# Agent values at a batch's end: the chain cut into five steps, with VectorE's part of each half moved behind other work

## The chip, the cores and the metric

The kernel runs on one core of one Trainium2 chip (trn2). The metric is the device time of one launch in microseconds. Before the change the median of three timed runs is 715.16 us (714.91 to 716.64).

## What is computed

The reference is agent attention followed by a mixture of experts. Four batches of N = 11456 rows of C = 128 numbers (q, k and v) and 49 agents a batch:

```python
a2k = sm(agents, k)              # softmax over the N keys, scale 1/sqrt(128)
agent_v = a2k @ v                # 49 x 128 a batch: the "agent values"
q2a = sm(q, agents)              # softmax over the 49 agents
x = (q2a @ agent_v).reshape(B * N, C)
do_compute = x @ w_skip > 0      # the other rows keep x
e_idx = argmax(x @ w_gate)       # one of 8 experts a row, gate_w its softmax weight
y = gate_w * (relu(x @ w1[e]) @ w2[e])
out = x + y where do_compute else x
```

`agent_v` of a batch needs all keys and values of that batch, and every query of the batch needs `agent_v`. So there are four points, one at each batch's end, at which a short serial chain (`agent_values`) turns a sum in PSUM into the matrix `av` that the queries are multiplied with.

## The kernel before

**Two parts.** `attention` (about the first 312 us of the profile) works through 60 chunks, 15 a batch, of up to six columns of 128 rows each. `experts` (from about 345 us on) runs the gathered rows through the eight experts, one block of 384 rows at a time. The change touches `attention` alone.

**Slots.** `attention` is emitted as a list of 79 slots (0 to 78), and each engine runs its instructions in exactly the order in which they are emitted. In a slot of the steady state one chunk of queries goes through (scores `sQ`, maximum `qS`, exponential `qE`, transpose `qT`, product with `av` `mX`, division `qN`, gate `qG`, weight `qD`, output `qO`, each some slots behind the other), and in the same slots the keys (`sK`, `kC`, `kM`, `vS`, `vE`) and values (`vA`) of the next batch. A slot has up to two key chunks (the first half of a batch) or two to three value chunks (the second half). The table `ORDER` says in which order a slot emits these stages, with one row a phase: "k" and "v" for batch 0's keys and values, "w" for slots 10 to 55, "q" for the last batch's queries from slot 56 on.

**Words that step helpers.** Some chains are Python generators in a list `back`; the word `bg` of a row advances each of them by one step, up to its next `yield`. Before, `bg` stands twice in a "w" slot and once in a "q" slot. Two sorts of generator matter here: `agent_values`, and `early`, which looks up rows for the experts and shares its slots with batch 2's chain. The word `rt` advances the routing work (`codes`, `count`, `routing`: the VectorE instructions named `best`, `code`, `mask`, `cum`, `oin`, `n`).

**The chain** `agent_values(b)` has three steps before. Step 1, called at once when the last value chunk is emitted (`vA`, slots 10, 25, 40 and 55): two VectorE copies `pa<-ps_a` (L432) of the summed products. Step 2, in the next slot's first `bg`: TensorE's product with `pairs` (L435) adds the two halves, and VectorE copies the result to `at` (L437). Step 3, in the second `bg` of that slot (a "q" slot later for batch 3): three TensorE products (L440 to L442) into a PSUM tile `pv`, then VectorE's sum, reciprocal and two scalings (L445, L446, L449) that write `av`.

```python
vec.tensor_copy(pa[h : h + NA, :], st["A"][h : h + NA, : C + 1])
yield
ten.matmul(pt[:, :P], lhsT=pa[:, :C], rhs=pairs, start=True, stop=True)
vec.tensor_copy(at, pt[:, :P])
yield
ten.matmul(pv[:, :C], lhsT=at, rhs=ident, start=True, stop=True)
```

**Names in the rows.** `ps_s` are the three PSUM tiles of scores, `qm` (L456) is VectorE's maximum over a query chunk, `qe` (L462) ScalarE's exponential of it, which frees the `ps_s` tile, `eT` (L472) ScalarE's copy of the transposed exponentials (L470), `ps_x` (L483) the product with `av`, and L491, L499 the division on VectorE that ends in `xs` and `G`. `top` (L520) on VectorE, a subtraction on GpSimd (L521) and `best` (L551) on VectorE belong to the gate. `ps_e` are two PSUM tiles that the transposes and the chain share. Loads go through SyncE's queue into 13 buffers (`ld`, `more`, `lds`).

Of the kernel before, what the change touches and what calls it, by code (L numbers as in the profile page):

```python
# [44 lines left out]

ORDER = {
# [4 lines left out]
}  # L51


# [121 lines left out]
def attention(nc, tc, sh, io, ps):  # L175


    q, k, v, agents, w_skip, w_gate, w1, w2, flat = io
# [6 lines left out]
    chunks = [(b, ci) for b in range(sh.B) for ci in range(NCH)]  # L185
    with ExitStack() as ctx:
# [4 lines left out]
        rt = ctx.enter_context(tc.tile_pool(name="rt", bufs=1))  # L191
# [50 lines left out]
        while at < sh.NC:  # L242
            n = next((n for n in range(1, sh.NC - at) if sh.COLS[at + n] != sh.COLS[at] + n), sh.NC - at)
# [57 lines left out]
        def raw(e, i):  # L301

            src = w2[e].rearrange("(f p) d -> p f d", p=P) if i else w1[e]
            to = ps.raw[e][i].rearrange("p (f d) -> p f d", d=C) if i else ps.raw[e][i]
            behind(nc.sync.dma_start(out=to, in_=src), room(e))
# [40 lines left out]
        def weights(n):  # L346

            e, i = n
            tl, r = taken(("w", n))
            if i < 2:  # L350
                hi, lo = (x[:, i * 512 : (i + 1) * 512].rearrange("p (a b) -> p a b", b=C) for x in ps.w1[e])
            else:
                hi, lo = (x[:, (i - 2) * 4 : (i - 1) * 4, :] for x in ps.w2[e])
            r.append(act.copy(hi, tl))
            r.append(pool.tensor_tensor(out=lo, in0=tl, in1=hi, op=ALU.subtract))
            del held["w", n]
            yield
# [56 lines left out]
        def values(n):  # L414


            b, ci, cols, m = geometry(n)
            x = stored(n)
            tl, r = taken(("v", n))
            if ci == 0:  # L420
                st["A"] = ps_a.tile([P, 512], F32, name="ps_a")
            for t in range(m):
                h = 64 * (t % 2)
                r.append(ten.matmul(st["A"][h : h + NA, : C + 1], lhsT=x[:, t, :], rhs=tl[:, t, :],
                                    start=(ci == 0 and t < 2), stop=(ci == NCH - 1 and t >= m - 2)))
            st["last"] = r
            del held["v", n]

        def agent_values(b):

            for h in (0, 64):
                vec.tensor_copy(pa[h : h + NA, :], st["A"][h : h + NA, : C + 1])  # L432
            yield
            pt = ps_e.tile([P, 512], F32, name="ps_e")
            ten.matmul(pt[:, :P], lhsT=pa[:, :C], rhs=pairs, start=True, stop=True)  # L435
            at = one.tile([P, P], F32, name="at")
            vec.tensor_copy(at, pt[:, :P])  # L437
            yield
            pv = ps_e.tile([P, 512], F32, name="ps_e")
            ten.matmul(pv[:, :C], lhsT=at, rhs=ident, start=True, stop=True)  # L440
            ten.matmul(pv[:, C : C + NE + 1], lhsT=at, rhs=wgs, start=True, stop=True)
            ten.matmul(pv[:, W - 1 : W], lhsT=pairs, rhs=pa[:, C:], start=True, stop=True)  # L442
            rs = one.tile([P, 1], F32, name="rs")
            av = avs[b % 2]
            vec.tensor_scalar(rs, pv[:, W - 1 : W], EPS, None, op0=ALU.add)  # L445
            vec.reciprocal(rs, rs)  # L446
            for h in (0, 64):
                s = slice(h, h + NA)
                vec.tensor_scalar(av[s, : W - 1], pv[s, : W - 1], rs[s], None, op0=ALU.mult)  # L449
            st["av", b] = av  # L450
# [354 lines left out]
        def static(upto):  # L805

            n = 0
            while st["items"] < upto:
                f, *args = items[st["items"]]
                n += f in (rows, layer1, first_result)  # L810
                waits = {layer2: (layer1, *args), first_result: (sums, 0)}.get(f)
                if n > 2 or any(i == waits or f in (rows, layer1) and i[0] is rows for i, _ in open_):
                    return
                g = iter(f(*args))
                if next(g, True) is None:
                    open_.append(((f, *args), g))
                st["items"] += 1
# [11 lines left out]
        def goal(kind, i):  # L829
            lst = {"k": sh.K, "v": sh.V, "q": range(1 - sh.Q0, n_all + 1)}[kind]  # L830
            return max(0, lst[min(i, len(lst) - 1)]) if i >= 0 else 0
# [12 lines left out]
        def prefetch(i):  # L844
            nonlocal pos
            while pos < len(order) and order[pos][0] < i + 8:
                bufs = few + (i < late + PAR["few"][0]) * rooms + (i < late + PAR["few"][1]) * many[-PAR["more"] :]
                if not free(bufs):
                    break
                load(order[pos][1], bufs)  # L850
                pos += 1

        back, fresh, queue = [], [], []

        def step(lst, n=None):
            for g in lst[:n]:
                if next(g, True):
                    lst.remove(g)
# [13 lines left out]
        def values_done(n):  # L872
            assert done["vE"] > n
            values(n)
            if chunks[n][1] == NCH - 1:
                begin(agent_values(chunks[n][0]))

        def begin(g):
            next(g)
            fresh.append(g)  # L880
# [30 lines left out]
        def held_up(x, n):  # L911
            return ("mb", chunks[n][0]) not in st if x == "vS" else done["vS"] <= n
# [9 lines left out]
        with tc.manual_schedule(engines=None):  # L922
            for i in range(slots):
                prefetch(i)
                back += fresh
                fresh.clear()
                at = i - sh.Q0
                phase = "k" if i < -(-NCH // PAR["first"]) + 1 else "v" if at < 0 else "w" if i < sh.LATE else "q"
                if at in EARLY:
                    assert st["routed"] >= 0  # L930
                    back.append(early(EARLY[at]))
                for n in starts.get(i, []):
                    wgen.append(weights(n))
                for n in raws.get(i, []):
                    raw(*n)
                for word in ORDER[phase].split():
                    x, soft, lag = word[:2], word.endswith("?"), int(word[2:].strip("?") or 0)
                    if x == "bg":
                        step(back)
                    elif x == "rt" or x == "rx" and at >= n_all - 4:  # L940
                        step(queue, 1)
                    elif x == "wt":
                        step(wgen)
                    elif x == "rx":
                        pass
                    elif x == "sa":
                        static(STATIC.get(at - n_all, len(items) if at > n_all else 0))
                    elif x in ("sr", "sx"):
                        for pair in open_[:]:
                            if next(pair[1], True) or x == "sx":  # L950
                                open_.remove(pair)
                    else:
                        kind, f = stages[x]
                        to = goal(kind, i - lag)
                        if x == "kM" and goal(kind, i + 1) % NCH == 0:
                            to = goal(kind, i)
                        while done[x] < to and not (soft and held_up(x, done[x])):
                            f(done[x])
                            done[x] += 1
            assert all(x == n_all for x in done.values()) and not open_ and st["items"] == len(items), done  # L960
            back += fresh
            assert not wgen
            while back:
                step(back)
            while queue:
                step(queue, 1)
# [566 lines left out]
def build(nc, args, out, n):  # L1533
    sh = Shapes(args[0].shape[0], n)
    ps = Persist(nc, sh)
    io = args + [out]
    with tile.TileContext(nc) as tc:
        attention(nc, tc, sh, io, ps)
    experts(nc, sh, out, ps)
# [32 lines left out]
```

## Time and profile before

| what | before |
|---|---|
| median of three timed runs | 715.16 us |
| fastest and slowest of them | 714.91, 716.64 us |
| the profiled execution's own time | 708.03 us |
| its span, first to last instruction | 706.5 us |
| TensorE matmul busy | 630.2 us (89%) |
| VectorE busy | 518.1 us (73%) |
| ScalarE busy | 359.8 us (51%) |
| GpSimd busy | 194.5 us (28%) |
| mean granted TensorE clock | 0.948 |

Busy times are of the span of the profiled execution. In the rows below PE is TensorE's matmuls, PEld its weight loads, DVE VectorE, ACT ScalarE, POOL GpSimd and SP SyncE. "[2.16 <-PE ps_a L424]" behind a row means that the engine sat idle for 2.16 us just before it and that a TensorE instruction of line 424 ended the wait. The granted clock is given as a share: 1.00 is 2.4 GHz and 0.50 is 1.2 GHz. Line numbers in these rows are those of the kernel before; in the changed file those behind L435 are one or two higher.

### The profile page before, as it was taken

What the parts mean: (1) busy time and instruction counts of PE and PEld (TensorE: products, weight loads), DVE (VectorE), ACT (ScalarE), POOL (GpSimd) and SP (SyncE); (2) the same over time, 40 slices, a digit from 0 to 9 for tenths busy, and PEclk for the clock granted to TensorE, in tenths of its full rate; (3) what the DMA queues carried; (4) which work ended last, traced back from release to release, by engine and by line L of the source; (5) the groups of instructions that cost most, each with busy time, mean ns of one, the idle gap of its engine ahead of it and who ended that gap; (6) DMA issues with size and microseconds to landing.
All of it is one profiled execution on the core that took longest, in us unless ns stands there. A gap on an engine that the chain in (4) does not pass through costs nothing. (4 is left out here: it accounts for less than half of the span.)

```text
span 706.5 us, 21190 instructions
## 1 busy us (share of the span) xinstructions
PE 630.2 (89%) x6808; PEld 583.9 (83%) x6808; DVE 518.1 (73%) x1854; ACT 359.8 (51%) x1024; POOL 194.5 (28%) x322
## 2 busy tenths in 40 slices
PE   6599898798888979977787999999999999999985
PEld 6588787687777867766676899999999999999985
DVE  4527568876877688876555878888888888888884
ACT  3336565465344545642434455555555555555552
POOL 2302440252234412145554531111111101011253
PEclk9799999989797989997999999999999999999998
DMA  8999899999797999621121101111111111111100
GB/s 315 358 360 375 287 402 404 401 308 404 271 343 256 372 379 318 233 101 48 43 42 36 35 29 47 46 47 46 47 46 46 35 37 44 47 46 52 42 25 5
DMA packets 56760, 119.69 MB, mean 169 GB/s; under 512 B 12902, under 2 KB 21226, under 8 KB 56624
## 3 DMA queue, kind: packets, MB, share of 16 engines
q1 hardware_dynamic: 42064, 79.92, 32.1%
q10 hardware_dynamic: 8928, 23.79, 8.6%
q0 software_dynamic: 5632, 14.53, 6.6%
q14 instruction: 95, 0.78, 0.4%
q8 instruction: 41, 0.67, 0.4%
HBM read 87.18 MB, written 31.50 MB: 168 GB/s over the span
## 5 line engine op out<-in xcount | busy, mean ns | idle before, releaser
L1308 ACT ACTIVATE hh<-h 128x384 fp32r<-128x384 f32 x296 | 143.7, 491 | 107.6 <-ACTq L996 101.4
L1243 DVE SCALAR_TENSOR_TENSOR hl<-h,hh 128x384 fp32r<-128x384 f32 x296 | 155.3, 552 | 41.8 <-DVEq L996 30.9
L1484 PE MATMUL y<-hh,w 128*128 128x384 f32 x592 | 160.0, 351 | 15.4 <-PEq L996 14.5
L1478 PE MATMUL h<-xh,w 128*128 128x384 f32 x592 | 154.0, 342 | 4.4 <-PEq L996 4.4
L1484 PEld LDWEIGHTS y<-hh,w 128*128 128x128 f32 x592 | 102.7, 190 | 20.4 <-issue 20.2
L1478 PEld LDWEIGHTS h<-xh,w 128*128 128x128 f32 x592 | 108.9, 191 | 5.5 <-issue 5.5
L1478 PE MATMUL h<-xl,w 128*128 128x384 f32 x296 | 101.1, 342 | 0.0
L1484 PE MATMUL y<-hl,w 128*128 128x384 f32 x296 | 100.3, 339 | 0.0
L462 ACT ACTIVATE qe<-ps_s,qm 128x49 f32<-128x49 f32 x360 | 75.2, 308 | 39.2 <-DVE qm L456 34.5
L1354 POOL DMA_DIRECT2D xg<-out_dram x29 | 15.8, 543 | 203.2 <-issue 203.1
L483 PE MATMUL ps_x<-av,eT 50*128 50x138 f32 x720 | 62.0, 307 | 8.2 <-DVE G L499 8.0
L483 PEld LDWEIGHTS ps_x<-av,eT 50*128 50x128 f32 x720 | 49.5, 196 | 19.8 <-issue 9.1
L366 PE MATMUL ps_s<-agT,ld 128*64 128x49 f32 x1296 | 50.8, 236 | 11.5 <-DMA ld<-in_k_dram 5.6
L366 PEld LDWEIGHTS ps_s<-agT,ld 128*64 128x64 f32 x1296 | 45.9, 150 | 17.2 <-issue 12.5
L499 DVE TENSOR_TENSOR xs<-ps_x,qr 128x768 f32<-128x768 f32 x60 | 57.5, 959 | 3.5 <-DMA out_dram<-xs 0.6
L1478 PEld LDWEIGHTS h<-xl,w 128*128 128x128 f32 x296 | 56.6, 191 | 0.0
L1484 PEld LDWEIGHTS y<-hl,w 128*128 128x128 f32 x296 | 55.8, 189 | 0.0
L1304 ACT ACTIVATE yT<-y 128x384 f32<-128x384 f32 x37 | 18.1, 491 | 65.8 <-ACTq L996 58.9
L407 POOL TENSOR_TENSOR scores<-scores,mb 128x294 f32<-128x294 f32 x53 | 41.6, 811 | 29.1 <-DVE mb L401 24.7
L374 ACT COPY scores<-ps_s 128x294 f32<-128x294 f32 x60 | 23.9, 420 | 43.3 <-PE ps_s L366 35.3
L366 PE MATMUL ps_s<-agT,lds 128*64 128x49 f32 x1056 | 41.2, 231 | 5.0 <-issue 2.9
L366 PEld LDWEIGHTS ps_s<-agT,lds 128*64 128x64 f32 x1056 | 36.6, 145 | 10.0 <-issue 5.7
(200 smaller groups left out, 1005.5 us busy)
## 6 DMA issues: line engine op xcount, KB each, us to landing
out_dram<-xs ACTq DMA_DIRECT2D x60, 387.0 KB, 6.9
ld<-in_q_dram SPq DMA_DIRECT2D x29, 384.0 KB, 7.4
ld<-in_k_dram SPq DMA_DIRECT2D x25, 384.0 KB, 7.8
lds<-in_v_dram SPq DMA_DIRECT2D x24, 387.0 KB, 6.6
lds<-in_k_dram SPq DMA_DIRECT2D x23, 384.0 KB, 7.5
lds<-in_q_dram SPq DMA_DIRECT2D x21, 384.0 KB, 7.3
ld<-in_v_dram SPq DMA_DIRECT2D x20, 387.0 KB, 6.4
more<-in_v_dram SPq DMA_DIRECT2D x16, 387.0 KB, 7.2
```

Source lines behind the costliest of these rows:

```text
L366: r.append(ten.matmul(pt[h : h + 64, t * NA : (t + 1) * NA], lhsT=xT[:, t * P + h : t * P + h + 64], rhs=agT[:, b, :], start=True, stop=True))
L374: act.copy(stored(n), s)
L407: eng.tensor_tensor(out=x, in0=x, in1=st["mb", chunks[n][0]].unsqueeze(1).to_broadcast(x.shape), op=ALU.subtract)
L462: act.activation(qes[n % PAR["qe"]][:, t, :NA], s[:, t, :], AF.Exp, bias=mx[:, t : t + 1])
L483: ten.matmul(px[:, h, t, :], lhsT=eT[s, t * P : (t + 1) * P], rhs=st["av", b][s, :], start=True, stop=True)
L499: vec.tensor_tensor(out=out, in0=px[:, :, :, w], op=ALU.mult, in1=rs.unsqueeze(3).to_broadcast(list(px[:, :, :, w].shape)))
L1243: v.scalar_tensor_tensor(out=hl[:, f], in0=h_ps[f % HB], scalar=0.0, in1=hh[:, f], op0=ALU.max, op1=ALU.subtract).then_inc(sem["HL"], 1)
L1304: s.activation(yT, y_ps, AF.Copy).then_inc(sem["YS"], 1)
L1308: s.activation(hh[:, f], h_ps[f % HB], AF.Relu).then_inc(sem["HH"], 1)
L1354: g.dma_start(out=xg[n % TURN].rearrange("p h c -> p (h c)"), in_=in_rows(n)).then_inc(x, 16)
L1478: w = t.matmul(h_ps[f % HB], lhsT=ps.w1[e][wx][:, cs], rhs=x, start=(n == 0), stop=(n == 2))
L1484: w = t.matmul(y_ps, lhsT=ps.w2[e][wx][:, f, :], rhs=h[:, f], start=(f == 0 and n == 0), stop=(f == FC - 1 and n == 2))
```

## The change

`agent_values` gets two more `yield`s, so that it has five steps: copies to `pa`; the `pairs` product; the copy to `at`; the three products into `pv`; `av`. A new word `be` at the place of the last `bg` of a "v", "w" or "q" slot also takes up chains that were put into a new list `ended`. The chain is put there when the last value chunk is emitted, and no longer started at once. So step 1 comes at the end of its slot, TensorE's steps at the next two slots' `bg`, and VectorE's steps at the same slots' `be`. In the "q" row `bg` moves ahead of `qS`, and `be` takes its old place.

```diff
-    "w": "qN+4 sK kC vS-1? qD+5 sQ+1 vA vE-1? bg qS+1 qG+4 qE+1 kM+1 rt qT+2 qO+5 mX+3 bg vS-1 vE-1 rt wt",
-    "q": "sr qN+4 qD+5 sQ+1 sx qS+1 sa qG+4 qE+1 bg qT+2 rt qO+5 mX+3 rt rx wt",
+    "w": "qN+4 sK kC vS-1? qD+5 sQ+1 vA vE-1? bg qS+1 qG+4 qE+1 kM+1 rt qT+2 qO+5 mX+3 be vS-1 vE-1 rt wt",
+    "q": "sr qN+4 qD+5 sQ+1 sx bg qS+1 sa qG+4 qE+1 be qT+2 rt qO+5 mX+3 rt rx wt",
...
             ten.matmul(pt[:, :P], lhsT=pa[:, :C], rhs=pairs, start=True, stop=True)
+            yield
             at = one.tile([P, P], F32, name="at")
             vec.tensor_copy(at, pt[:, :P])
             yield
...
             ten.matmul(pv[:, W - 1 : W], lhsT=pairs, rhs=pa[:, C:], start=True, stop=True)
+            yield
             rs = one.tile([P, 1], F32, name="rs")
...
-                begin(agent_values(chunks[n][0]))
+                ended.append(agent_values(chunks[n][0]))
...
                     if x == "bg":
+                        step(back)
+                    elif x == "be":
+                        back += ended
+                        ended.clear()
                         step(back)
```

No instruction is added or dropped. ScalarE's, GpSimd's and SyncE's orders stay as they are; TensorE's and VectorE's change at the four batch ends.

VectorE at batch 2's end (slot 40), before. `ehit` and `want` are of `early`, `qm` is the next query chunk's maximum, `best` is of the gate:

```order
L499 TENSOR_TENSOR G<-ps_x,qr 128x2x3x9
L432 COPY pa<-ps_a 49x129 x2
L700 TENSOR_SCALAR ehit<-iota,rank,rec 128x128 x3
L703 TENSOR_SCALAR want<-rank,rec 128x3
L704 TENSOR_TENSOR want<-want,rank 128x3
L456 TENSOR_REDUCE qm<-ps_s 128x6
L520 TENSOR_REDUCE top<-G 128x12
L551 SCALAR_TENSOR_TENSOR best<-G,desc 128x192
```

and with the change:

```order
L501 TENSOR_TENSOR G<-ps_x,qr 128x2x3x9
L702 TENSOR_SCALAR ehit<-iota,rank,rec 128x128 x3
L705 TENSOR_SCALAR want<-rank,rec 128x3
L706 TENSOR_TENSOR want<-want,rank 128x3
L458 TENSOR_REDUCE qm<-ps_s 128x6
L522 TENSOR_REDUCE top<-G 128x12
L553 SCALAR_TENSOR_TENSOR best<-G,desc 128x192
L432 COPY pa<-ps_a 49x129 x2
```

The copies that need the summed values have moved from ahead of `qm` to behind `best`. For batches 1 and 3 it is the same; for batch 0 they stay where they are.

TensorE in the two slots after batch 2's end (41 and 42), before; `ps_s` products are scores, `qe` transposes:

```order
L366 MATMUL ps_s<-agT,lds 64x49 x36
L435 MATMUL ps_e<-pairs,pa 128x128
L470 MATMUL ps_e<-ident,qe_110 128x128 x3
L483 MATMUL ps_x<-av_159,eT 128x138 x6
L440 MATMUL ps_e<-ident,at 128x128
L441 MATMUL ps_e<-wgs,at 128x9
L442 MATMUL ps_e<-pa,pairs 128x1
L366 MATMUL ps_s<-agT,lds 64x49 x12
L366 MATMUL ps_s<-agT,ld_95 64x49 x12
L366 MATMUL ps_s<-agT,lds 64x49 x12
```

and with the change:

```order
L366 MATMUL ps_s<-agT,lds 64x49 x36
L435 MATMUL ps_e<-pairs,pa 128x128
L472 MATMUL ps_e<-ident,qe_110 128x128 x3
L485 MATMUL ps_x<-av_159,eT 128x138 x6
L366 MATMUL ps_s<-agT,lds 64x49 x12
L366 MATMUL ps_s<-agT,ld_95 64x49 x12
L366 MATMUL ps_s<-agT,lds 64x49 x12
L441 MATMUL ps_e<-ident,at 128x128
L442 MATMUL ps_e<-wgs,at 128x9
L443 MATMUL ps_e<-pa,pairs 128x1
```

The three products that need `at` have moved behind the next slot's three groups of scores.

VectorE in slot 42, with the change (`run` is the keys' running maximum, `oin` and `n` are of the routing):

```order
L385 TENSOR_TENSOR run<-scores,run 128x294 x2
L577 MEMSET oin_3020 128x1
L578 COPY oin_3020<-cum_2941 128x8
L580 TENSOR_TENSOR n_3023<-oin_3020 128x8
L447 TENSOR_SCALAR rs<-ps_e 128x1
L448 RECIPROCAL rs<-rs 128x1
L451 TENSOR_SCALAR av_158<-ps_e,rs 49x137 x2
L553 SCALAR_TENSOR_TENSOR best<-G,desc 128x96
```

Before, the three rows that write `av` stood a slot earlier, behind the last row of `early` and ahead of the scan `cum`.

## Rows read from the trace of the kernel before

**Rows 1.** Busy time by stretch: length, PE, PEld, DVE, ACT, POOL busy, clock, DMA share, GB/s

```profile
103.50:170.00 66.50, 59.46 (x1143) 51.84 (x1141) 51.17 (x160) 36.53 (x144) 19.49 (x41) 0.95 1.00 376
170.00:246.00 76.00, 66.94 (x1146) 57.68 (x1143) 58.65 (x207) 36.46 (x142) 28.74 (x49) 0.87 0.89 319
345.00:706.00 361.00, 339.56 (x2045) 330.73 (x2043) 278.73 (x1083) 189.47 (x402) 83.95 (x109) 0.98 0.14 40
```

**Rows 2.** Timeline, VectorE's part of the chain: start us, length us, instruction [idle before]

```profile
43.42 0.60 DVE L432 COPY pa<-ps_a 49x129 f32<-49x129 f32 x2 [8.92 <-PE ps_a L424]
45.92 0.29 DVE L437 COPY at<-ps_e 128x128 f32<-128x128 f32 x1 [1.91 <-PE ps_e L435]
103.57 0.60 DVE L432 COPY pa<-ps_a 49x129 f32<-49x129 f32 x2 [1.60 <-PE ps_a L424]
108.13 0.29 DVE L437 COPY at<-ps_e 128x128 f32<-128x128 f32 x1 [0.45 <-PE ps_e L435]
110.13 0.16 DVE L445 TENSOR_SCALAR rs<-ps_e 128x1 f32<-128x1 f32 x1 [0.49 <-PE ps_e L442]
170.17 0.60 DVE L432 COPY pa<-ps_a 49x129 f32<-49x129 f32 x2 [2.16 <-PE ps_a L424]
177.37 0.29 DVE L437 COPY at<-ps_e 128x128 f32<-128x128 f32 x1 [1.13 <-PE ps_e L435]
181.06 0.16 DVE L445 TENSOR_SCALAR rs<-ps_e 128x1 f32<-128x1 f32 x1 [1.44 <-issue]
245.95 0.59 DVE L432 COPY pa<-ps_a 49x129 f32<-49x129 f32 x2 [1.45 <-PE ps_a L424]
```

**Rows 3.** Timeline, what stands behind the chain at batch 2's end

```profile
166.53 1.61 PE L366 MATMUL ps_s<-agT,ld 128*64 128x49 f32 x48
171.90 0.46 DVE L456 TENSOR_REDUCE qm<-ps_s 128x6 f32<-128x294 f32 x1
172.99 0.36 DVE L551 SCALAR_TENSOR_TENSOR best<-G,desc 128x192 bf16<-128x192 f32 x1 [0.47 <-POOL G L521]
174.48 2.13 PE L366 MATMUL ps_s<-agT,lds 128*64 128x49 f32 x48 [1.83 <-ACT qe L462]
```

**Rows 4.** Busy time by stretch of 4 us, columns as in rows 1

```profile
112.00:116.00 4.00, 2.71 (x61) 2.31 (x59) 3.78 (x13) 1.62 (x7) 0.50 (x1) 1.00 1.03 407
172.00:176.00 4.00, 2.17 (x66) 2.05 (x61) 3.35 (x13) 2.51 (x10) 0.67 (x3) 0.92 1.03 414
176.00:180.00 4.00, 4.00 (x31) 3.32 (x30) 2.33 (x12) 1.63 (x7) 0.09 (x1) 0.50 0.97 364
184.00:188.00 4.00, 3.81 (x65) 3.17 (x63) 3.79 (x16) 1.16 (x7) 1.24 (x2) 0.80 0.53 174
```

**Rows 5.** Timeline, TensorE's waits at the ends of batches 0, 1 and 3

```profile
46.27 0.49 PE L440 MATMUL ps_e<-ident,at 128*128 128x128 f32 x2 [0.38 <-DVE at L437]
114.09 0.97 PE L483 MATMUL ps_x<-av,eT 50*128 50x138 f32 x12 [1.29 <-DVE G L499]
249.52 0.55 PE L470 MATMUL ps_e<-ident,qe 128*128 128x128 f32 x3 [0.97 <-ACT eT L472]
```

**Rows 6.** Timeline, the same TensorE work, one chunk's scores, at either clock

```profile
171.75 0.91 PE L366 MATMUL ps_s<-agT,lds 128*64 128x49 f32 x24
182.27 1.49 PE L366 MATMUL ps_s<-agT,ld 128*64 128x49 f32 x24
```

**Rows 7.** Loads: two key loads' issue in SyncE's queue, and their kind's median time to landing

```profile
158.50 2.22 SPq L336 DMA_DIRECT2D lds<-in_k_dram  x2
...
lds<-in_k_dram SPq DMA_DIRECT2D x23, 384.0 KB, 7.5
```

**Rows 8.** Timeline, batch 2's `av`, routing's `n`, and the first product with that `av`

```profile
181.45 0.74 DVE L449 TENSOR_SCALAR av<-ps_e,rs 49x137 f32<-49x137 f32 x2
187.50 0.17 DVE L578 TENSOR_TENSOR n<-oin 128x8 bf16<-128x8 f32 x1
190.54 0.98 PE L483 MATMUL ps_x<-av,eT 50*128 50x138 f32 x12
```

More of the change, by code (lines that the diff above doesn't have):

```diff
@@ L851, in prefetch @@
                 pos += 1
-        back, fresh, queue = [], [], []
+        back, fresh, ended, queue = [], [], [], []
         def step(lst, n=None):
```

2 rows, old and new, of the table ORDER are left out of this document.

## The prediction

> **What bounds the kernel now.** I read the busy time by stretch first. The experts' part (the last row of [rows 1]) is TensorE's, 339.56 us busy of 361, and the change does not touch it: whatever attention gains or loses shifts this part as a whole. In attention no engine is alone at its limit: from 103.5 to 170 us TensorE is busy 59.46 us of 66.5 and VectorE 51.17, with transfers at 376 GB/s; the next batch takes 76 us, at a mean clock of 0.87 instead of 0.95. So I looked at the four batch ends for the wait that ends last.
>
> The timeline of VectorE shows it [rows 2]. At each batch's end VectorE comes to the two copies to `pa` and sits idle until TensorE has finished the value products: 8.92, 1.60, 2.16 and 1.45 us for batches 0 to 3. It runs its instructions in order, so what stands behind the copy waits too. At batch 2 that is `qm`, the query chunk's maximum. Its scores are among the 48 products that begin at 166.53 and take 1.61 us, so they are there by 168.2; `qm` starts at 171.90 [rows 3]. ScalarE's exponentials wait for `qm`, the `ps_s` tile is free only after them, and TensorE stands still for 1.83 us until 174.48 "<-ACT qe". Then the clock falls: 1.00 before, 0.92 over 172 to 176, where TensorE is busy 2.17 us of 4, and 0.50, the 1.2 GHz level, from 176 to 180 [rows 4].
>
> **The change, part by part.** Nothing is added, so every term is a wait that goes or a piece of work that lies elsewhere. The sum is made against the profiled execution (708.03 us); the timed median is 715.16, 7.13 us or 1% above it, which no row explains, and I carry the difference over as it is. A gain of one slot counts once, since all later slots follow.
>
> *Copies to `pa` behind `best`, batches 1 to 3.* VectorE gets to `qm` without the wait. By the time `best` is done, TensorE has ended the value products, so the wait goes and is not put off: at batch 2 VectorE is free at 168.0 (170.17 less 2.16). `ehit` and `want` take the 1.1 us between the copies' end (170.77) and `qm` (171.90), `qm` 0.46, and `top`, GpSimd's subtraction and `best` the 1.0 us up to 173.35 [rows 2, 3]: it reaches the copies at about 170.6, 0.4 us after TensorE let them go.
>
> *`pairs` and `at` parted.* The copy to `at` waits 1.91, 0.45, 1.13 and 0 us now [rows 2], none for batch 3, since TensorE's product comes only just before it. Behind `qm`, `run`, `code` and `mask` it has no wait left. TensorE's products that need `at` move behind three groups of scores, 2.7 us at full clock (3 x 0.91, [rows 6]), so TensorE is no longer kept by `at` either.
>
> *`av` at the end of the next slot.* The waits of 0.49 and 1.44 us ahead of L445 [rows 2] go the same way. The work itself, 0.16 + 0.16 + 0.74, some 1.1 us, stays and lies a slot later. The `ps_e` tile that holds `pv` is kept about a slot longer; only a transpose two tiles on needs it, and that one stands behind a slot of scores, so I cost it at nothing (if that cover failed, 1 to 2 us a batch).
>
> *The word moved in "q".* It touches batch 3's chain alone: the three `pv` products go ahead of a static block's transposes. Nothing waits for either there; 0.
>
> The terms, batch by batch:
> - Batch 0: the copies stay. TensorE's own wait for `at`, 0.38 us [rows 5], goes. Bounds 0 and 1.91 (all of VectorE's wait for `pairs`). I take **0.4**, TensorE's row, since VectorE idles 8.92 us just before and is no limit there.
> - Batch 1: VectorE's waits are 1.60 + 0.45 + 0.49 = 2.54 us. Part of it VectorE will spend on waiting for TensorE's scores and products instead, since it comes to them earlier. TensorE has a wait of 1.29 us on VectorE's `G` in the same slots [rows 5]. Bounds 0 and 2.54; I take **1.2**, just under the nearest row, 1.29.
> - Batch 2: VectorE's waits are 2.16 + 1.13 + 1.44 = 4.73 us, and VectorE is the limit afterwards (3.79 us busy of 4 from 184 to 188, [rows 4]), so what it saves is worth most here. On TensorE's side the stall is 1.83; without it the clock need not fall, and at 0.50 a chunk's scores take 1.49 us instead of 0.91 [rows 6]: the two chunks left of slot 41 and the three of slot 42 lose 5 x 0.58 = 2.9 us, and with the transposes and products among them I put the slow stretch at 3.3 us, an estimate. Bounds 1.8 (the stall alone) and 4.73. I take the middle, **3.3**, because both engines must be early for a slot to be early, and the clock's share is not certain.
> - Batch 3: VectorE's wait is 1.45 us, TensorE waits 0.97 us for `eT` in the slot behind [rows 5], which hangs on `qm` in the same way. Bounds 0 and 1.45; **0.9**, by TensorE's row.
>
> Sum: 0.4 + 1.2 + 3.3 + 0.9 = **5.8 us**: 702.2 us for a profiled execution like this one, 715.16 - 5.8 = **709.4 us** for the median.
>
> **The rivals.**
>
> *The slow stretch comes anyway.* From 112 to 116 us TensorE is busy 2.71 us of 4 and the clock stays at 1.00; from 172 to 176 it is busy 2.17 and the clock falls [rows 4]. So it is a matter of degree, and the profiled run and the timed ones differ by 1%, more than this whole term. If the clock falls there all the same, batch 2 gives back what the low level costs and keeps some 1.0 us: 0.4 + 1.2 + 1.0 + 0.9 = 3.5, **711.7 us**. The Trainium skill (TensorE: Matmul & The Clock Gate, section on the clock gate) says that the monitor behind the clock runs on a beat of its own that is not tied to the kernel, and that the same kernel meets it at another point from run to run. By that rule the 3.3 us is a draw and not a saving. One trace cannot show it; the two rows above do not contradict it.
>
> *The transfers hide it.* At 112 to 116 and 172 to 176 the transfer engines are busy throughout (share 1.03) at 407 and 414 GB/s, the most in these rows. If data were the limit, an earlier VectorE would only wait for loads: no gain, **715.2 us**. For it speaks that share; against it, that the two key loads issued from 158.50 on are read at 171.75 and 174.48, 13 us after their issue, where the median to landing is 7.5 [rows 3, 6 and 7], and that the rate falls to 174 GB/s from 184 to 188 [rows 4], with buffers full.
>
> *`av` comes too late (slower).* Now batch 2's `av` is done at 182.19, and its first use, a product on TensorE, is at 190.54: 8.4 us of room [rows 8]. With the change `av` stands behind `n`, which ends at 187.67, and takes 1.1 us: at the pace of before 188.8, 1.7 us ahead of its use. If VectorE, the limit in that slot, falls more than 1.7 us behind TensorE, the product waits, the scores behind it wait in TensorE's order, and the clock may fall as it did at 174. For batches 1 and 2 a stall of 2 us and a slow stretch of 3.3 each make 10.6, less 5.8 gained: **720 us**. Against it speaks that everything ahead of `av` on VectorE also comes earlier, by more than 1.7 us at batch 2.
>
> That the change does not do what it says can be left aside: the orders show each row moved as described.
>
> **How the numbers follow.** I give my forecast 0.53, the slow stretch that comes anyway 0.14, the transfers 0.21 and the late `av` 0.12. About 0.3%, 2.1 us, is what a measurement of this kernel can tell from no change. The first two lie below 713.0, so faster is 0.67; the third is within it, same 0.21; the fourth slower, 0.12. The range: all upper bounds together are 1.91 + 2.54 + 4.73 + 1.45 = 10.6 us, 704.5; upward it takes in the case of the transfers with the scatter of the runs before, which reaches 1.48 us above their median: 716.5. The late `av` is left out.
>
> **What would show it.** In the profile of the changed kernel, `pa` of batches 1 to 3, `at` and L447 (the old L445) should have no idle time worth naming ahead of them; that of batch 0's `pa` stays near 8.9 us. The stall of 1.83 us "<-ACT qe" behind batch 2's end should be gone and the clock there be 1.00; the stretch from batch 2's end to batch 3's (170 to 246 now) should be shorter by some 3 us, the one before it by about 1, and the experts' part unchanged. I am wrong if VectorE's idle time goes and the batch ends do not move (transfers, or TensorE), if a low clock turns up at another place, or if the first product with a new `av` waits for it.

## The result, and the profile after

| what | before | after |
|---|---|---|
| median, first comparison | 715.28 us (714.91 to 716.64, 4 runs) | 705.06 us (704.27 to 706.48, 4 runs) |
| the profiled execution's own time | 708.03 us | 704.27 us |
| its span | 706.5 us | 702.7 us |
| mean granted TensorE clock | 0.948 | 0.949 |

The ratio is 0.990, with a 95% interval of [0.986, 0.9939]. Two later comparisons, with more runs, gave 0.9917 [0.9889, 0.9945] (705.74 against 712.21 us) and 0.9906 [0.9877, 0.9934] (705.43 against 712.46 us). So the change gains about 6 to 7 us. (The ratios are not the quotients of the two medians and differ from them by up to 0.003.) The 10.2 us between the first two medians also hold a draw of the kernel before: over 34 runs of it in a later comparison the median is 712.5 us, and the time went from 706.89 us, at a mean clock of 0.958, to 715.91 us, at 0.935. Runs more than 1.5% above the fastest of their kernel are left out of the ratios; here that is a 35th run of 717.78 us.

The timeline of VectorE in the changed kernel answers to [rows 2]; L438 and L447 are the old L437 and L445:

```profile
42.39 0.60 DVE L432 COPY pa<-ps_a 49x129 f32<-49x129 f32 x2 [7.93 <-PE ps_a L424]
50.12 0.16 DVE L447 TENSOR_SCALAR rs<-ps_e 128x1 f32<-128x1 f32 x1 [1.46 <-PE ps_e L443]
103.53 0.60 DVE L432 COPY pa<-ps_a 49x129 f32<-49x129 f32 x2 [0.46 <-PE ps_a L424]
108.38 0.28 DVE L438 COPY at<-ps_e 128x128 f32<-128x128 f32 x1
112.89 0.15 DVE L447 TENSOR_SCALAR rs<-ps_e 128x1 f32<-128x1 f32 x1
168.02 0.59 DVE L432 COPY pa<-ps_a 49x129 f32<-49x129 f32 x2
173.78 0.28 DVE L438 COPY at<-ps_e 128x128 f32<-128x128 f32 x1
179.22 0.15 DVE L447 TENSOR_SCALAR rs<-ps_e 128x1 f32<-128x1 f32 x1
179.61 0.74 DVE L451 TENSOR_SCALAR av<-ps_e,rs 49x137 f32<-49x137 f32 x2
238.95 0.60 DVE L432 COPY pa<-ps_a 49x129 f32<-49x129 f32 x2
```

The waits of 1.60, 2.16 and 1.45 us ahead of the copies are 0.46, 0 and 0, and those ahead of `at` and `rs` of batches 1 and 2 are gone. Batch 0 keeps its long wait, and ahead of its `rs` VectorE waits 1.46 us, where it waited 0.33 before; the last section shows what TensorE did there. TensorE's timeline behind batch 2's end answers to [rows 3]:

```profile
165.69 2.16 PE L424 MATMUL ps_a<-more,scores 128*49 128x129 f32 x36
...
169.45 2.32 PE L366 MATMUL ps_s<-agT,lds 128*64 128x49 f32 x72
...
182.32 0.97 PE L485 MATMUL ps_x<-av,eT 50*128 50x138 f32 x11
...
186.47 1.17 PE L366 MATMUL ps_s<-agT,more 128*64 128x49 f32 x24 [1.61 <-ACT qe L464]
```

The three groups of scores of slot 41 are one row now, without the 1.83 us ahead of the second. A stall "<-ACT qe" of 1.61 us comes further on, in slot 44. The kernel before has one at the same place, shorter, and its clock stays at 1.00 from 188 to 196 us:

```profile
193.54 0.91 PE L366 MATMUL ps_s<-agT,more 128*64 128x49 f32 x24 [1.19 <-ACT qe L462]
```

The busy time of the same stretches as in [rows 4] (PE, PEld, DVE, ACT, POOL, then clock, DMA share and GB/s):

```profile
172.00:176.00 4.00, 3.50 (x83) 3.07 (x83) 3.81 (x13) 2.34 (x9) 1.84 (x1) 1.00 1.03 399
176.00:180.00 4.00, 3.53 (x64) 3.01 (x59) 3.74 (x18) 1.32 (x8) 1.88 (x3) 1.00 1.03 404
184.00:188.00 4.00, 2.39 (x61) 2.27 (x62) 3.73 (x15) 2.39 (x10) 0.97 (x2) 0.87 1.03 389
```

The clock is 1.00 where it was 0.92 and 0.50. From 184 to 192 us it falls instead, behind the 1.61 us stall: 0.87 in the last row, and 0.71 from 188 to 192. VectorE is busy 3.7 to 3.8 us of every 4: from the end of the copies on it has next to no idle time until 188 us. The experts' part does the same work; this stretch of 361 us begins 6.8 us earlier, as its first block does:

```profile
338.20:699.20 361.00, 340.49 (x2052) 332.34 (x2051) 279.63 (x1084) 190.47 (x405) 82.92 (x108) 0.99 0.13 40
```

But it is not as long as before. The stretch in [rows 1] ends 0.5 us ahead of the end of the span, this one 3.5 us. From the start of the first block, shown below, to the end of the span the profiled execution of the kernel before took 378.7 us and that of the changed kernel 381.6; the twelve further executions in this document, one of them of the kernel before, took 381.0 to 383.2. So the execution that the prediction was worked out from was some 3 us short in a part that no edit touches. This is why the profiled executions lie only 3.8 us apart although attention ends 6.8 us earlier. Of these 6.8 us, 1.0 lie ahead of batch 0's end (41.21 against 40.19 below), where nothing was changed.

To see which batch's end gave what, I take the start of TensorE's last value products of each batch as a milestone. In the kernel before, by its timeline:

```profile
41.21 2.16 PE L424 MATMUL ps_a<-ld,scores 128*49 128x129 f32 x36
...
102.03 1.49 PE L424 MATMUL ps_a<-ld,scores 128*49 128x129 f32 x24
...
167.96 2.16 PE L424 MATMUL ps_a<-more,scores 128*49 128x129 f32 x36
...
243.75 2.16 PE L424 MATMUL ps_a<-lds,scores 128*49 128x129 f32 x36
...
327.83 0.98 PE L1478 MATMUL h<-xh,w 128*128 128x384 f32 x2 [2.83 <-PEq L996]
```

and in the changed one:

```profile
40.19 2.16 PE L424 MATMUL ps_a<-ld,scores 128*49 128x129 f32 x36
...
101.99 1.49 PE L424 MATMUL ps_a<-ld,scores 128*49 128x129 f32 x24
...
236.75 2.16 PE L424 MATMUL ps_a<-lds,scores 128*49 128x129 f32 x36
...
321.07 0.98 PE L1484 MATMUL h<-xh,w 128*128 128x384 f32 x2 [2.58 <-PEq L1002]
```

The differences of these starts, with the same ones from the profiles of the experiments below (one execution each):

| profile | batch 0 to 1 | 1 to 2 | 2 to 3 | 3 to first expert block |
|---|---|---|---|---|
| before | 60.82 | 65.93 | 75.79 | 84.08 |
| before, once more (e1_same) | 59.43 | 65.30 | 77.88 | 82.49 |
| after | 61.80 | 63.70 | 71.06 | 84.32 |
| after, once more (e8_after) | 59.44 | 66.97 | 70.33 | 84.21 |
| after, once more (e13_after) | 60.19 | 64.37 | 73.29 | 83.93 |
| copies alone (e2_pa) | 61.31 | 64.77 | 72.30 | 83.71 |
| copies alone (e12_pa) | 59.78 | 66.39 | 73.03 | 84.08 |
| copies alone, batch 2 alone (e9_pa2) | 59.35 | 67.53 | 71.44 | 85.23 |
| whole change, batch 2 alone (e4_b2) | 61.12 | 65.86 | 72.98 | 85.35 |
| whole change, batches 1 to 3 (e6_b123) | 61.91 | 62.12 | 73.39 | 83.80 |
| five steps alone (e3_five) | 61.76 | 64.45 | 74.86 | 84.63 |
| stall filled (e5_fill) | 61.41 | 64.39 | 75.21 | 82.96 |

Equal code differs by up to 3.3 us in the second column between two executions, so one row of it proves little. The third column is clear: with the copies of batch 2 moved it is 70.33 to 73.39, without 74.86 to 77.88. (The two experiments that move the look-ups are left out.)

A shorter stretch has less scatter. From the start of slot 40's query scores to the start of slot 42's it is 16.3 and 17.0 us in the two executions of the kernel before, and 9.8 in each of the three of the changed one; 10.5 to 10.6 with the copies alone, 13.4 with the five steps alone, 12.6 with the stall filled. To slot 46's it is 36.7 and 38.6 us before, 32.1, 32.2 and 33.7 after; 32.3 to 33.7 with the copies alone, 35.3 with the five steps alone, 35.9 filled. At batch 3's end the query scores of slots 55 and 57 begin, before:

```profile
243.02 0.91 PE L366 MATMUL ps_s<-agT,lds 128*64 128x49 f32 x24
...
250.90 0.91 PE L366 MATMUL ps_s<-agT,ld 128*64 128x49 f32 x24
```

and after:

```profile
236.02 0.91 PE L366 MATMUL ps_s<-agT,lds 128*64 128x49 f32 x24
...
242.71 0.91 PE L366 MATMUL ps_s<-agT,ld 128*64 128x49 f32 x24
```

That is 7.9 and 6.7 us. Of the executions in the table, every one without batch 3's copies moved has 7.9 and every one with them 6.7.

### The profile page after: what moved, and what is told of

Read it like the earlier page. It is cut to its first block, busy times and chain, and to the rows that moved or that the text cites. A ratio compares the mean times of both kernels' runs of the same rounds, so it can differ in the third digit from the quotient of the medians.

```text
span 702.7 us, 21183 instructions
## 1 busy us (share of the span) xinstructions
PE 627.1 (89%) x6808; PEld 582.6 (83%) x6808; DVE 519.0 (74%) x1854; ACT 359.4 (51%) x1024; POOL 195.4 (28%) x322
## 5 line engine op out<-in xcount | busy, mean ns | idle before, releaser
L1490 PE MATMUL y<-hh,w 128*128 128x384 f32 x592 | 161.8, 355 | 17.0 <-PEq L1002 14.5
L1490 PEld LDWEIGHTS y<-hh,w 128*128 128x128 f32 x592 | 104.3, 192 | 21.5 <-issue 21.3
L366 PEld LDWEIGHTS ps_s<-agT,ld 128*64 128x64 f32 x1296 | 46.8, 153 | 15.5 <-issue 10.2
L366 PEld LDWEIGHTS ps_s<-agT,lds 128*64 128x64 f32 x1056 | 34.8, 141 | 8.8 <-issue 6.1
L366 PE MATMUL ps_s<-agT,lds 128*64 128x49 f32 x1056 | 38.8, 227 | 3.3 <-issue 2.9
```

The costliest lines, as they stand in the source:

```text
L366: r.append(ten.matmul(pt[h : h + 64, t * NA : (t + 1) * NA], lhsT=xT[:, t * P + h : t * P + h + 64], rhs=agT[:, b, :], start=True, stop=True))
L1490: w = t.matmul(y_ps, lhsT=ps.w2[e][wx][:, f, :], rhs=h[:, f], start=(f == 0 and n == 0), stop=(f == FC - 1 and n == 2))
```

## The experiments

**The kernel before against itself.** No edit.

> The kernel before, unchanged, as a control: its profiled execution took 708.03 us and its timed runs 714.91 to 716.64. If executions of this kernel fall into two levels some 7 us apart, single runs here lie near 708 and near 715; if the profiled one was a stray, all lie at 715 within 0.3%. My theory (the change saves what the profile shows, 6.8 us up to the first block of the experts) needs the first, since the medians differ by 10.2 us; the rival, that the timed runs before lose some 3 us more in the experts' part, would show in this run's blocks.

Measured: 0.9997 [0.9964, 1.003], 710.8 us against 712.5. Its 12 runs lie between 707.89 us (clock 0.952) and 716.05 (0.937). So the 7.13 us between the profiled execution and the median of before, which the prediction carried over unexplained, lie within the kernel's scatter from run to run, and its ends go with the clock. The expectation's rival came out too: in this profiled execution the first block of the experts begins 2.2 us earlier than in the one that the prediction read, and the span is 1.8 us longer, so the experts' part took 3.9 us more:

```profile
325.68 0.98 PE L1478 MATMUL h<-xh,w 128*128 128x384 f32 x2 [2.53 <-PEq L996]
```

The mean clock was higher in it (0.954 against 0.948), so the clock does not explain that part; what does stays open.

**The move of the copies alone.**

```diff
-    "w": "... mX+3 bg vS-1 vE-1 rt wt",
+    "w": "... mX+3 be vS-1 vE-1 rt wt",
...
-                begin(agent_values(chunks[n][0]))
+                ended.append(agent_values(chunks[n][0]))
```

The last `bg` of a "v" or "w" slot and the one `bg` of a "q" slot become `be`; the chain keeps its three steps.

> Only the copies to pa are moved (to the end of their slot, batches 1 to 3), the rest of the chain in three steps as before. Theory that the wait ahead of qm is what costs: VectorE's waits that go are 5.2 of 8.7 us, and TensorE's stall of 1.83 us at batch 2's end goes with them, so 6 to 7 of the 10.2 us, near 709. Rival, that the waits at the copy to at and at av cost: within 3 us of before, 712 to 715.

Measured: 0.9901 [0.987, 0.9932], 705.16 us. Run once more beside the changed kernel:

> The move of the copies alone (batches 1 to 3, chain of three steps), once more, beside the changed kernel on one chip. If the five steps add nothing once the copies stand behind best: within 0.15% of the changed kernel, 0.990 to 0.993 of before. If they carry a part of their own: slower than the changed kernel by 0.3% or more.

Measured: 0.9901 [0.986, 0.9941], 707.43 us over 7 runs (701.4 to 712.2), with 705.43 for the changed kernel. The medians are 0.28% apart, between the two forecasts of 0.15 and 0.3%, and within the scatter of 7 and 6 runs; the ratios are nearly equal (0.9901 and 0.9906). The times alone do not decide whether the five steps add something. The timeline of VectorE at batch 2's end in the first of these runs:

```profile
168.94 0.59 DVE L432 COPY pa<-ps_a 49x129 f32<-49x129 f32 x2
173.14 0.29 DVE L437 COPY at<-ps_e 128x128 f32<-128x128 f32 x1 [0.35 <-PE ps_e L435]
175.31 0.15 DVE L445 TENSOR_SCALAR rs<-ps_e 128x1 f32<-128x1 f32 x1
```

and its busy time there:

```profile
172.00:176.00 4.00, 4.00 (x81) 3.63 (x77) 3.39 (x17) 2.03 (x8) 0.64 (x3) 1.00 1.04 407
176.00:180.00 4.00, 2.88 (x61) 2.50 (x57) 3.89 (x11) 0.72 (x2) 0.94 (x1) 1.00 1.02 399
```

Nothing was done about `at` and `rs`, yet their waits of 1.13 and 1.44 us are 0.35 and 0, and the clock is 1.00. At batch 2 these two waits were a consequence of the stall, or of the low clock behind it, and not a cause of their own; the stall filled with work, below, tells which.

**The five steps alone**, with the copies where they were.

```diff
+            yield
             at = one.tile([P, P], F32, name="at")
...
+            yield
             rs = one.tile([P, 1], F32, name="rs")
```

The words of the table are as in the whole change, but the chain still begins at once.

> The five steps without the move: the copies to pa stay where they were, the copy to at and av lie later. Theory of the wait ahead of qm: 2 to 4 us less than before, 711 to 713, and TensorE's stall of 1.8 us at batch 2's end and the 1.2 GHz stretch behind it are still there. Rival, that at and av are what counts: 6 to 8 us less, 707 to 709.

Measured: 0.9944 [0.9919, 0.9969], 708.8 us. TensorE's timeline shows the stall, at the size it had before:

```profile
173.15 2.27 PE L366 MATMUL ps_s<-agT,lds 128*64 128x49 f32 x48 [1.83 <-ACT qe L464]
```

and in the busy time the clock falls behind it, for a shorter time than before (it falls once more from 188 to 196 us, to 0.86 and 0.50, behind a stall of 2.34 us in slot 44):

```profile
172.00:176.00 4.00, 2.85 (x51) 2.76 (x52) 3.27 (x14) 2.21 (x10) 0.32 (x2) 0.73 1.03 406
176.00:180.00 4.00, 4.00 (x88) 3.54 (x86) 3.81 (x13) 2.17 (x9) 2.19 (x1) 0.84 0.95 323
```

So the stall hangs on the copies alone. By the ratio the five steps are worth some 4 us (1.8 to 5.8 by its interval) while the copies stall VectorE: in this trace neither `at` nor `rs` of batch 2 has a wait. They are not added to the copies' 7 us. With the copies moved, the five steps bring slot 42 forward by another 0.8 us (9.8 against 10.5 to 10.6 from slot 40 on), and by slot 46 nothing of that can be seen.

**The whole change at batch 2 alone.** `ended` and the new `yield`s are used where `b` is 2.

> The whole change at batch 2's end alone, the others as before. Theory that this end holds most of the gain, through the clock: 4 to 6 us less than before, 709 to 711, with a clock of 1.00 behind the batch's end. Rival, that the ends give about the same each: 2 to 3 us less, 712 to 713.

Measured: 0.9937 [0.9909, 0.9965], 708.67 us, 4.5 us less than before by the ratio. **The copies alone, at batch 2 alone:**

> Only the copies to pa, and only those of batch 2, are moved to the slot's end; the chain has three steps as before. Theory 1 (batch 2's gain is qm no longer waiting behind the copies, and the clock that stays up for it): TensorE's stall of 1.83 us gone, clock 1.00 for 10 us behind batch 2's end, slots 45 to 48 earlier by 4 to 4.5 us against slot 40, as with the copies of three batches moved (4.4), time 0.993 to 0.995 of before, like the whole change at batch 2 alone (0.9937). Theory 2 (batches 1 and 3 carry as much as batch 2): 0.997 or more. Theory 3 (the parted pairs, at and av are needed at batch 2): the stall comes back at another place of slots 41 and 42, and no more than 1 us is left by slot 45.

Measured: 0.9938 [0.9914, 0.9961], 706.48 us: the same ratio again. By the ratios (0.0062 of 712, 4.4 us) batch 2's copies carry about two thirds of the whole; by the medians of their comparison it is 5.7 us of the 6.5 that the changed kernel gains there. So they carry most of it, and how much is left for the other batches is not settled. Its TensorE timeline shows slot 41 without the stall, and a wait for VectorE a slot later:

```profile
171.50 2.32 PE L366 MATMUL ps_s<-agT,lds 128*64 128x49 f32 x72
...
180.40 0.98 PE L483 MATMUL ps_x<-av,eT 50*128 50x138 f32 x12 [1.11 <-DVE G L499]
```

**The stall filled with work.** This is the kernel before, which here repeats a chunk's score products twice, 48 rows more, ahead of the stall; its line numbers from there on are 6 higher.

```diff
+                    if (kind, n) == ("k", 46) and t == m - 1 and h:
+                        for u in range(2 * m):
+                            for g in (0, 64):
+                                r.append(ten.matmul(pt[g : g + 64, u % m * NA : (u % m + 1) * NA],
...
```

> The kernel before, with one edit: behind the chunk of key scores that TensorE does just ahead of its 1.83 us stall at batch 2's end, the same chunk's products are done twice more (48 rows of the trace, some 1.6 us by 0.91 us for 24 of them), so that TensorE computes where it stood still. The wait of qm behind pa, and every other order, stay. Theory 1 (most of batch 2's gain is the clock that no longer falls; the stall only sets it off): no idle time of more than 0.4 us ahead of the next scores, clock 1.00 over the 10 us behind it, the slots behind earlier by 2 to 3 us, time 0.996 of before (709.5 where before is 712.5). Theory 2 (the stall itself is the gain, and the clock falls by itself somewhere near): the next scores start at the same time as before, a low clock within the next 10 us all the same, time 0.999 to 1.002 of before.

Measured: 0.9981 [0.9955, 1.0006], 709.52 us, which doesn't tell the theories apart. The trace does, for the place itself. TensorE:

```profile
170.69 1.57 PE L371 MATMUL ps_s<-agT,lds 128*64 128x49 f32 x48
172.70 1.61 PE L366 MATMUL ps_s<-agT,lds 128*64 128x49 f32 x48 [0.44 <-ACT qe L468]
```

VectorE:

```profile
168.38 0.60 DVE L438 COPY pa<-ps_a 49x129 f32<-49x129 f32 x2 [2.15 <-PE ps_a L430]
174.76 0.29 DVE L443 COPY at<-ps_e 128x128 f32<-128x128 f32 x1 [0.31 <-PE ps_e L441]
176.94 0.15 DVE L451 TENSOR_SCALAR rs<-ps_e 128x1 f32<-128x1 f32 x1
```

and the busy time:

```profile
176.00:180.00 4.00, 3.66 (x81) 3.25 (x81) 3.79 (x12) 1.96 (x8) 1.25 (x1) 1.00 1.00 379
180.00:184.00 4.00, 2.10 (x42) 1.83 (x42) 3.79 (x17) 1.09 (x6) 1.37 (x2) 0.93 1.01 372
184.00:188.00 4.00, 3.60 (x53) 3.18 (x53) 3.09 (x13) 1.43 (x5) 1.57 (x5) 0.50 0.33 119
```

The copies still make VectorE wait 2.15 us, but TensorE computes meanwhile, and the clock is 1.00 for 10 us more; `at` and `rs` wait 0.31 and 0 us. So it is the idle TensorE that brings the clock down there, and the low clock that makes `at` and `rs` late. Then, as VectorE bounds the next slots (3.79 of 4), TensorE idles again, busy 2.10 of 4, and the clock falls to 0.50 all the same. The stretch from batch 2's end to batch 3's is 75.21: theory 1 holds for 10 us, and by this one execution theory 2 for the sum.

**Batch 0 as before, the rest changed**, and the changed kernel beside it:

> The whole change for batches 1, 2 and 3; batch 0 keeps the chain of three steps with its copies at once. In the changed kernel batch 0's end came out 1.1 us later by slot 14 than before, and no gain of it was left by slot 25. Theory 1 (the five steps gain nothing at batch 0): the same time as the whole change, within 0.2%, 0.989 to 0.992 of before. Theory 2 (they cost at batch 0, where TensorE gets a low clock right behind the chain): slots 14 to 22 earlier by 1 us than in the changed kernel, and this kernel faster than the whole change by 0.1 to 0.2%, 0.988 of before. Theory 3 (batch 0's five steps carry a part): 0.993 or more.

> The changed kernel as it is, once more, on the chip and beside the runs of the other three, as their yardstick. The move of the copies alone had 0.990 of before with 712.5 us for before. If the five steps add to that what they gained alone (0.994), 0.986 or less, 702 us; if the gains of the two parts are one and the same (the batch ends' waits), 0.989 to 0.991, 704.5 to 706 us. By the forecast's sum, 5.8 us, 0.992.

Measured: 0.9905 [0.9874, 0.9937] (704.28 us, 6 runs) and 0.9917 [0.9889, 0.9945] (705.74 us, 12 runs). The intervals overlap; batch 0's five steps gain nothing that can be seen here, and whether they cost anything stays open.

**What bounds the slots behind batch 2's end now.** If VectorE does, its work there must go elsewhere. `early`, the look-up for the experts, has two of its four starts in these slots.

```diff
-EARLY = {30: 0, 32: 1, 38: 2, 40: 3}
+EARLY = {26: 0, 28: 1, 38: 2, 40: 3}
```

> The changed kernel, and the first two of the four early look-ups for the experts start in slots 36 and 38 (value slots) instead of 40 and 42 (batch 2's end). In the changed kernel VectorE has no idle time from slot 40 to 43, and the look-ups are some 3 us of VectorE's work each and hold one of the three score tiles for half a slot. Theory 1 (with the waits gone, VectorE's work bounds the slots behind batch 2's end): slots 40 to 44 shorter by 2 to 4 us, and TensorE no longer waits for qe there; 0.995 of the changed kernel or less. Theory 2 (transfers, at a share of 1.03 there, bound these slots next): TensorE waits for loads instead, no more than 0.5 us is gained, 0.999 to 1.001 of the changed kernel. Theory 3 (what slots 40 to 44 gain, slots 36 to 39 lose, since VectorE idles only 1.5 us in each): within 0.2% too, but with the loss to be seen ahead of slot 40.

> The changed kernel once more, as the yardstick of the other three: 0.990 to 0.993 of before, 705 to 707 us, by the two comparisons so far.

Measured: 700.95 us (698.54 to 705.09), 0.9859 [0.9825, 0.9892] of before, with 705.43 us, 0.9906 [0.9877, 0.9934], for the changed kernel in the same comparison: 4.5 us less by the medians, 3.3 by the ratios, and the fastest version here. Slots 36 to 39 lost about 1 us. TensorE's timeline and busy time behind batch 2's end, changed kernel first:

```profile
186.79 1.52 PE L366 MATMUL ps_s<-agT,more 128*64 128x49 f32 x24 [1.60 <-ACT qe L464]
```

```profile
180.00:185.00 5.00, 4.08 (x87) 3.46 (x87) 4.71 (x18) 1.52 (x6) 1.56 (x4) 1.00 1.04 386
185.00:190.00 5.00, 3.40 (x58) 3.19 (x54) 3.44 (x15) 2.48 (x10) 1.33 (x4) 0.58 0.96 367
```

and with the look-ups moved:

```profile
183.25 0.91 PE L366 MATMUL ps_s<-agT,ld 128*64 128x49 f32 x24 [0.17 <-ACT qe L464]
```

```profile
180.00:185.00 5.00, 4.52 (x96) 3.82 (x96) 4.79 (x19) 2.66 (x11) 0.93 (x4) 1.00 1.03 398
185.00:190.00 5.00, 4.95 (x119) 4.38 (x117) 4.24 (x16) 2.87 (x13) 0.62 (x2) 1.00 1.03 399
```

The stall of 1.60 us is 0.17, and the clock stays at 1.00 in these 10 us; it falls a little later here too, to 0.89 over 192 to 196. The transfers were at their full share in both, so they did not bound these slots. A look-up takes VectorE's time and, by the expectation above, holds one of the three score tiles for half a slot. Both left these slots together, so this run does not tell which of the two counted.

**All look-ups later**, in slots 48 to 54 (`EARLY = {38: 0, 40: 1, 42: 2, 44: 3}`):

> The changed kernel, and all four early look-ups start in slots 48, 50, 52 and 54 (value slots of the next batch) instead of 40, 42, 48 and 50. By theory 1 of the run before this one slots 40 to 44 come out shorter by 2 to 4 us without a loss ahead of them; if slots 48 to 55 can hide two more look-ups, 0.995 of the changed kernel; if they can't (VectorE idles 2.2 to 3 us of 5 in part of them, but 0.2 to 0.7 in others), half of it comes back there. If the look-ups come too late for the first static blocks of the experts, the stretch from slot 57 on gets longer, 1.00 or more.

Measured: 0.9899 [0.9869, 0.9929], 704.85 us, no different from the changed kernel. Against the kernel before, its query scores of slot 40 begin 0.8 us earlier and those of slot 46 9.9 us earlier; from slot 52 to slot 56 the lead shrinks from 11.0 to 5.6 us: in this execution the look-ups cost there about what they cost at batch 2's end.

## Why the prediction was right, and where it wasn't

The measured gain, 0.990 with its later 0.9917 and 0.9906, agrees with the 5.8 us of the sum, which make 0.992. The median of 705.06 us is 4.3 us below the 709.4 of the forecast and lies 0.6 us inside the range (whose upper end, 715.16 and 1.48, should read 716.6). The mechanism at batch 2's end was right. That the sum came out as well is in part luck: the traces put batch 2 above its term and batches 0 and 1 below theirs, with a scatter as large as these terms. By its own steps:

- *What bounds the kernel now: `qm` behind the copies at batch 2's end.* Right: the copies moved alone give the whole gain as far as the times can tell, and without that move the stall is 1.83 us as ever.
- *Copies to `pa` behind `best`.* Right, but for 0.46 us that are left at batch 1 in this execution. VectorE was to come to them 0.4 us after TensorE let them go; at batch 2 TensorE's products run to 167.85 and the copies begin at 168.02, 0.2 us later and without a wait.
- *`pairs` and `at` parted, and `av` a slot later.* The waits go at batches 1 and 2, as forecast, but not the one ahead of batch 0's `rs`, and this step had the cause wrong at batch 2: 0.8 us of the 1.13 and all of the 1.44 go when the copies alone are moved, or when TensorE is merely kept busy. They were TensorE being late at the low clock. The parting is a second way to the same gain.
- *Batch 2, 3.3 us* is the term that was mis-sized. By the third column of the table it is 76.8 less 71.6, some 5.3 us (means of two and of three executions), a little above the upper bound of 4.73; from slot 40 to slot 46 it is 37.6 less 32.7, 5.0 us. The ratios of the two runs at batch 2 alone make it 4.4 to 4.5, with intervals that take in 3.3, so the traces show the size better than the times do. I took the middle "because both engines must be early"; in fact VectorE, busy 3.7 to 3.8 us of 4, set these slots, and it saved all it had waited. In the second execution of the kernel before the low clock also lasted longer than in the one I read (0.50 throughout from 172 to 188 us).
- *Batches 0, 1 and 3, together 2.5 us.* Batch 1: 65.6 less 65.0, 0.6 against 1.2. Batch 0: 60.1 less 60.5, nothing against 0.4. Batch 3: 83.3 less 84.2, a loss of 0.9 against a gain of 0.9, with equal code 1.6 apart. None can be told from zero over so long a stretch. At batch 3's end itself the gain is there, 1.2 us from slot 55 to slot 57 in every execution, close to the 0.9 of the forecast; what the slots behind it do with it is lost in the scatter. By the ratios, the 2 to 3 us that the copies of all batches bring beyond those of batch 2 are batches 1 and 3 together, and they are no more certain than those intervals.
- *The rival of the slow stretch that comes anyway* was half right, and one of the prediction's own signs of being wrong, "a low clock turns up at another place", did show. The low clock left its place, but in the changed kernel it comes again from about 187 us on, behind the 1.61 us stall, and e13_after and e5_fill show it there too. In the profiled execution it is shorter than before (0.87 and 0.71 over two stretches of 4 us, where it was 0.92, 0.50, 0.50 and 0.80 over four), and it does not take back the gain. Against the execution of before that the prediction read, the changed kernel gains 6.5 us from slot 40 to slot 42 in each of its executions; by slot 46 that is 3.0 in e13_after and 4.5 in the other two. The Trainium skill (TensorE: Matmul & The Clock Gate, Part 1 on the clock gate) ties the clock to how busy TensorE has recently been, and the runs agree: where the idle time was filled or removed, the clock stayed up at that place (1.00 from 176 to 180 us, where it was 0.50).
- *The transfers* did not hold it: at the same share of 1.03 the slots became shorter, with e10_early26 once more.
- *`av` too late:* batch 2's `av` ends at 180.35 and its first product begins at 182.32, 2.0 us of room where 1.7 were forecast. It did not decide.
- *The experts' part unchanged.* Right by the second execution of the kernel before (382.6 us against 381.6 to 383.2); the one that the prediction read was 3 to 4 us short there. This and the scatter are behind the 7.13 us that were carried over.
- *The medians.* Of the 10.2 us about 3 are not the change's: they are the first comparison's four runs of before, at 714.91 to 716.64 us, where later runs have a median of 712.5. From there the forecast's 5.8 us would lead to 706.7.

## What to carry to other kernels

On an engine that runs in order, a short copy that waits for another engine's last result holds up everything behind it; put it behind work that is ready, and cutting the chain further may then be unnecessary. When one stall brings a slower clock, later waits in the same trace may be its consequences: remove the first wait alone before counting the others as gains of their own. After such a repair, look at once for what bounds the same slots next: here moving side work of VectorE, and the score tile that it held, out of them was worth another 3 to 4.5 us. And time a change against several runs and more than one trace of the kernel before: one execution here was 3 us short in a part that nobody touched.

## What the runs showed of the hardware that was not expected

- The same kernel spreads over 9 us from run to run (706.89 to 715.91), and the slower runs have the lower mean clock (0.958 in the fastest, 0.935 in the slowest). Which of the two brings the other was not tried.
- Part of the spread is not in the clock: the experts' part took 378.7 us in one execution and 382.6 in another of the same kernel, at mean clocks of 0.948 and 0.954.
- In the slots after batch 0's end TensorE stops between two instructions of the same line, for nothing that the profile shows. In the changed kernel:

```profile
49.81 0.27 PE L443 MATMUL ps_e<-pa,pairs 128*128 128x1 f32 x1 [1.96 <-issue]
...
50.40 2.80 PE L366 MATMUL ps_s<-agT,ld 128*64 128x49 f32 x48
```

  The 48 products behind it took 2.80 us, against 1.61 where the stop was 0.70 us (e13_after) or 0.57 (e8_after); with 1.70 us in e3_five they took 2.48. From 50 to 54 us the granted clock is 0.57 and 0.62 in the two with the longer stop, and 1.00 in the two with the shorter. The kernel before has such a stop, of 0.75 us, between two score products a little later. This is where the changed kernel's 0.4 us at batch 0 went in the profiled execution; what causes the stop was not tried.
